# Another written-out step order, with new operation and queue tables, for the opening part of a state-space and gated-MLP kernel

## The chip, the cores and the metric

The kernel runs on one core of one Trainium2 chip. The metric is the device time of one execution in microseconds; the kernel before has a median of 1714.06 us over three executions (1711.05, 1714.14 and 1714.06). The engines are called PE (matrix products), DVE, ACT, POOL and SP in the profile; POOL and SP issue most of the DMAs in the part that changes.

## The reference

A vector `c` makes six rows of modulation. The input `x` (2048 tokens, 576 channels) passes a state-space convolution and then a gated MLP, both with layer norm, modulation and a residual:

```python
mod = (_silu(c) @ w_mod).reshape(c.shape[0], 6, 1, -1)
h = _layernorm(x, axis=-1) * (1 + ca) + sa
P = jnp.exp(logdA[:, :, None] * l[None, None, :])          # 576 x 128 states x 2048 steps
K = jnp.einsum("dn,dnl,dn->dl", Cc, P, dB).real            # one long filter for each channel
x = x + ga * (irfft(rfft(h) * rfft(K)) + h * Dskip)
h = _layernorm(x, axis=-1) * (1 + cb) + sb
z = _gelu(h @ w_in); z1 = z[..., :2304]; z2 = _layernorm(z[..., 2304:])
g = w_sp @ z2 + b_sp
x = x + gb * ((z1 * g) @ w_out)
```

Here `irfft(rfft(...))` stands for the zero-padded Fourier product over 4096 points that the reference spells out.

## The kernel before

The program has three parts: `ssm` makes the filter, convolves, adds the residual and starts the MLP; `phase_a` takes 16 tiles of 128 tokens through the `z2` half of `w_in`; `phase_b` does the gate and the output. The change is in tables that `ssm` reads and in one loop of `phase_a`.

`ssm` consists of small functions, its steps, each issuing a handful of instructions. The list `ORDER` (L186 to L244) names all 1214 of them with their arguments, and the loop at L1003 calls them in that order. A wrapper, `Pin` (L147), keeps every instruction in program order on its engine, so each engine's queue is exactly the list read from left to right; every instruction made that way has line L152 in the profile, and groups are told apart by the names of their tiles. Three more tables belong to it. `GPQ` names the steps whose DMAs are issued by POOL; the others go to SP (`Q`, in `ssm`). `MODE` gives for each of 36 groups of 16 channels the way in which angles are reduced for sine and cosine. `COPY` gives for each group whether DVE ("1") or ACT ("0") copies its filter out of PSUM.

The steps, in the order in which data flows:

- `pole_in`, `pl`, `pload`: the state-space parameters are read, turned into exponents and phases split into bfloat16 parts, stored (`pb_d`, `pa_d`) and read back as `lb`, `lc` and `la`. `m_l`, `m_p`, `m_a`, `m_q`, `m_e`: one row of modulation each, from the load of `w_mod` through 12 products (`ps<-wm,ec`), an ACT copy (`mpart`), two products with `small`, to the result. `st_a`, `st_v`, `ln_r`, `ln_p`, `ln_a`: the layer norm of `x` with a first transform stage, stored to `u1_d`; its output tile is `st1o`.
- For each group: `e_p`, `e_a` (products `sel,lb`, exponential on ACT to `et`); `t_p` (L674, phases by products `sel,lc` and `sel,la`), `t_i`, `t_b` (reduction to a period, tile `ft`), `s_f`, `s_c` (sine and cosine on ACT); `p_a`, `p_b` (two DVE products `pg<-et,ft`) and `p_c` (two more, `et<-ft,et`); `kg_p` (32 matmuls `pk<-pg` and `pk<-et,pg`), `kg_a`, `kg_d`, `k1_p` and `k1_e` (L810, the copy to `k`).
- For each of five blocks of channels `c` and pieces `i`: `u_l`, `u_p`, `u_a` (the transformed input), `z_p` (products of `k` with `cst`), `z_m` (the DVE product `zz<-pk,uu`), `v_p` (products `zz,small`), `v_a` (copy and store to `v_d`). A `z_p` of a block can only come when all groups of that block (eight, in the last block four) have done `k1_e`.
- For each `c` and quarter `q` of the tokens: `y_v` (load of `v_d`; it needs all pieces of that block), `y_x` (load of `x`), `y_p` (L960, eight products with `st`, which are seen as 16 matmuls in the trace), `y_s` (L971, a DVE addition and the store of the new `x`). The data of `y_v.3.0` and `y_v.3.1` lie in `zz` tiles, that of `y_v.4.*` in `uu` tiles, all other in pairs of `u` tiles; block 4 is 64 channels wide, the others are 128 wide.
- `ml.*`, the start of the MLP: `start_load`, `start_sum`, `win_scale`, `start_hi`, `start_lo` for five column blocks of `w_in` (a power-of-two scale from a sum of squares, then a high and a low half-precision part, `wz`, from the tile `wst`); `ln2_stats`, `roots`, `ln2_rows` (second layer norm, tiles `bsx`, `mvx`, `n`), `turn` (transposes `ps<-ident,n` to `nt`), and `z2_mm`, `z2_gelu` of the first token tile (products `pk<-wz,nt`).

How a mode shapes a group's work: in mode 0 PE writes the phases alone, ACT adds a large constant that rounds them, and DVE subtracts (a SCALAR_TENSOR_TENSOR `ft<-ft,ps`) and clears signs. In the other modes PE does the rounding itself by adding and taking off the constant in products with `sel`, so the phases are accumulated twice:

```python
            if MODE[g]:
                magics(2112, True)
                phases((768, 0), False, False)
                magics(2240, False)
                phases((1536, 1792), False, True)
            else:
                phases((768, 0), True, True)
```

After that mode 1 takes a DVE copy and a mask, mode 2 a mask read straight from PSUM, mode 3 an ACT copy and a mask, and mode 4 an absolute value on ACT.

In `phase_a` (L1542) the loop at L1608 takes token tiles 1 to 15. Each has five chunks of products, `z2_mm(b, 0)` to `z2_mm(b, 4)`, each followed by its `z2_gelu`, and between them stand side works from lists (`sides`, called by `do(b, k)`): loads (LD), and the preparation of the other half of `w_in` and of later weights. For tile 1, A0 holds `side_sum(0)`, which squares and sums a block of `w_in` on ACT (`wso<-wst`), and PE holds `win_scale(0)`, which turns that sum into a scale by one small product and DVE work.

Of the kernel before, what the change touches and what calls it, by code (L numbers as in the profile page):

```python
# [170 lines left out]
u_a.1.0 u_a.1.2 u_a.1.4 u_a.2.0 u_a.2.1 u_a.2.3 u_a.2.4 u_a.3.2 u_a.3.4 u_a.3.5 u_a.3.6 u_a.4.0 u_a.4.1 u_a.4.3 u_l.0.0 u_l.0.3 u_l.0.6 u_l.0.7
u_l.1.0 u_l.1.2 u_l.1.3 u_l.1.5 u_l.1.6 u_l.1.7 u_l.2.2 u_l.2.5 u_l.2.6 u_l.2.7 u_l.3.1 u_l.3.2 u_l.3.3 u_l.3.4 u_l.3.6 u_l.4.0 u_l.4.3 v_a.0.2
v_a.0.6 v_a.0.7 v_a.1.1 v_a.1.3 v_a.1.4 v_a.1.5 v_a.1.7 v_a.2.0 v_a.2.1 v_a.2.3 v_a.2.4 v_a.2.5 v_a.3.1 v_a.3.3 v_a.3.4 v_a.3.7 v_a.4.0 v_a.4.1
v_a.4.2 wpre.1 x_l.1 x_l.3 y_s.0.0 y_s.0.1 y_s.1.0 y_s.1.1 y_s.2.1 y_s.2.2 y_s.3.0 y_s.4.0 y_s.4.1 y_s.4.3 y_v.0.0 y_v.0.1 y_v.0.3 y_v.1.0 y_v.1.1
# [4 lines left out]
pole_in.0.5 pole_in.0.4 pole_in.0.2 pole_in.0.1 pole_in.0.0 pl.0.0 pole_in.0.3 pole_in.0.6 pole_in.1.5 pole_in.1.0 pole_in.1.1 pl.0.1 pl.0.2 x_l.0
pl.0.3 pl.0.4 load.msk pl.0.5 pl.0.6 pl.0.11 pl.0.7 pl.0.8 pl.1.0 pl.1.1 pl.0.9 load.c pole_in.1.2 pl.1.2 mod_init st_a.0.0 pl.0.16 pl.0.13 m_l.2  # L180
m_p.2 pl.0.10 pl.0.17 st_a.0.1 st_a.0.2 pl.0.18 pl.0.12 pl.0.14 pl.0.15 m_l.0 m_p.0 st_a.0.3 st_a.0.4 load.small m_a.2 m_q.2 pload.0.0 m_a.0 m_q.0
pl.0.19 pl.0.20 pl.0.21 m_l.1 pl.0.22 pl.0.23 m_e.2 m_e.0 c_l.1 m_p.1 m_a.1 pole_in.1.3 load.sel e_p.1.0 e_p.3.1 pload.0.1 pl.1.11 m_q.1 m_e.1 e_p.4.1
r_l.0 ln_r.0 ln_r.1 e_a.1.0 c_l.0 r_l.1 ln_r.3 e_p.1.1 e_a.1.1 pload.0.2 x_l.1 r_l.2 m_l.3 t_p.1 t_i.1 st_v.1.0 st_v.1.1 t_p.0 load.dsk pole_in.1.4
t_i.0 e_p.2.0 ln_r.2 e_a.2.0 e_p.0.0 e_a.0.0 ln_p.0.0 ln_a.0.0 t_b.0 pole_in.1.6 r_l.3 pl.1.12 ln_p.0.1 t_b.1 s_f.1 ln_a.0.1 pl.1.3 st_v.1.2 pl.1.4
c_l.2 st_v.1.3 st_v.1.4 s_f.0 ln_r.5 ln_p.2.1 ln_a.2.1 ln_r.4 ln_p.2.0 ln_r.6 s_c.0 s_c.1 c_l.3 ln_a.2.0 e_p.0.1 ln_p.4.0 ln_a.4.0 pl.1.5 pl.1.6
e_a.0.1 x_l.2 ln_p.4.1 ln_a.4.1 pl.1.7 m_p.3 pl.1.8 pl.1.9 p_a.0 m_a.3 t_p.2 t_i.2 t_b.2 p_a.1 pl.1.10 p_b.1 p_c.1 ln_r.7 t_p.3 t_i.3 t_b.3 pl.1.16  # L186
s_f.2 p_b.0 p_c.0 kg_p.1 s_c.2 ln_p.6.0 e_a.3.1 ln_a.6.0 kg_a.1 st_v.2.0 st_v.2.1 pl.1.13 st_v.2.2 kg_d.1 e_p.3.0 st_v.2.3 e_a.3.0 m_l.4 e_p.2.1
e_p.5.1 e_a.5.1 ln_p.6.1 e_a.2.1 kg_p.0 ln_a.6.1 t_p.4 pl.1.14 r_l.4 m_q.3 e_a.4.1 t_i.4 kg_a.0 st_v.2.4 m_e.3 c_l.5 r_l.5 ln_r.11 p_a.2 ln_r.8 t_b.4
e_p.7.1 e_p.5.0 kg_d.0 c_l.4 e_a.5.0 e_p.4.0 m_p.4 e_a.4.0 p_b.2 k1_p.0 p_c.2 s_c.4 m_a.4 m_q.4 x_l.3 ln_r.9 s_f.4 k1_e.0 m_l.5 ln_r.10 s_f.3 pl.1.15
m_e.4 kg_p.2 kg_a.2 st_v.3.0 s_c.3 ln_p.8.0 kg_d.2 pl.1.17 st_v.3.1 ln_a.8.0 r_l.7 k1_p.1 e_p.6.1 e_a.6.1 ln_p.8.1 k1_p.2 ln_a.8.1 e_p.7.0 k1_e.2  # L190
e_a.7.0 e_a.7.1 t_p.5 t_i.5 m_p.5 p_a.4 st_v.3.2 k1_e.1 m_a.5 c_l.6 p_a.3 p_b.3 p_c.3 p_b.4 p_c.4 pload.1.0 t_p.7 t_i.7 pload.1.1 kg_p.3 kg_a.3 t_b.5
ln_p.10.0 ln_a.10.0 pl.1.18 t_b.7 s_c.5 ln_p.10.1 r_l.6 ln_a.10.1 pl.1.19 pl.1.20 e_p.6.0 t_p.6 t_i.6 e_a.6.0 s_f.5 st_v.3.3 e_p.9.1 st_v.3.4 e_p.14.1
ln_r.12 t_b.6 s_f.6 m_q.5 m_e.5 s_c.7 ln_r.15 kg_d.3 ln_r.13 s_c.6 p_a.5 kg_p.4 kg_a.4 c_l.7 ln_p.12.0 ln_a.12.0 k1_p.3 k1_e.3 s_f.7 ln_r.14 p_b.5
p_c.5 ln_p.14.1 ln_a.14.1 pl.1.21 pl.1.22 kg_p.5 p_a.6 pl.1.23 ln_p.14.0 ln_a.14.0 kg_a.5 e_a.9.1 ln_p.12.1 ln_a.12.1 e_p.11.1 e_a.11.1 e_p.8.1 turn
e_a.14.1 t_p.8 p_a.7 kg_d.4 pload.2.1 e_p.8.0 e_a.8.0 u_l.0.1 u_l.0.5 e_p.12.1 kg_d.5 u_l.0.4 u_l.0.2 t_i.8 p_b.7 p_c.7 e_a.8.1 e_p.9.0 pload.2.2
e_a.9.0 pload.1.2 p_b.6 p_c.6 t_b.8 s_f.8 k1_p.5 k1_e.5 k1_p.4 k1_e.4 u_l.0.0 s_c.8 t_p.10 t_i.10 t_p.9 t_i.9 cst_l.2 kg_p.6 kg_p.7 t_b.10 t_b.9 p_a.8
s_f.10 cst_l.0 kg_a.6 kg_d.6 s_c.10 kg_a.7 s_f.9 u_p.0.0 u_a.0.0 p_b.8 p_c.8 u_p.0.1 cst_l.1 k1_p.6 k1_e.6 s_c.9 p_a.9 kg_d.7 u_l.1.2 t_p.12 t_i.12
# [12 lines left out]
t_i.18 kg_d.17 t_b.18 s_c.18 s_f.18 u_p.1.4 z_p.1.1 z_m.1.1 kg_p.16 u_a.1.4 kg_p.20 kg_a.20 k1_p.17 s_f.19 k1_e.17 t_p.21 t_i.21 t_p.22 v_p.1.2 s_c.19  # L210
v_a.1.2 p_a.18 p_b.18 p_c.18 t_i.22 z_p.1.0 v_p.1.1 t_b.21 z_m.1.0 s_c.21 u_p.1.3 z_p.1.5 v_a.1.1 kg_a.16 u_l.1.6 s_f.21 u_a.1.3 v_p.1.0 kg_p.18
y_p.0.2 e_p.22.0 t_b.22 s_c.22 s_f.22 v_a.1.0 kg_d.20 e_p.21.0 z_m.1.5 pload.3.0 e_a.21.0 kg_d.16 u_l.1.7 p_a.19 k1_p.16 p_b.19 y_s.0.2 u_l.2.6
kg_a.18 p_c.19 e_a.22.0 k1_p.20 k1_e.20 k1_e.16 kg_d.18 k1_p.18 p_a.21 t_p.23 e_p.24.0 e_a.24.0 k1_e.18 p_b.21 p_c.21 e_p.22.1 e_a.22.1 z_p.1.4
# [2167 lines left out]
```

## Time and profile before

| | |
|---|---|
| median of three executions | 1714.06 us |
| the profiled execution | 1710.31 us |
| its span, first to last instruction | 1708.3 us |
| PE busy | 1644.1 us, 96% |
| DVE, ACT, POOL busy | 1244.0, 834.2, 250.1 us |
| granted PE clock, mean over the span | 0.978 |
| moved by DMA | 376.24 MB, 220 GB/s |

The prediction quotes rows of four kinds. The page's slices cut the span into 40 equal parts of 42.7 us, each a digit for tenths of busy time. A row of windows gives a stretch, its length and the busy time of PE, weight loads, DVE, ACT and POOL with instruction counts, then the granted clock as a share of full speed, the DMA share and GB/s. A row of the timeline gives start, duration (of the whole run of equal instructions), engine, line, operation, output tile, input tiles, shapes and count; the bracket is the engine's idle time before it and what ended that. A row of a group gives a count, then busy time, mean ns of one, and idle time with its releasers. Matmuls in a row overlap in the trace, so the time from one start to the next says more than the sum of durations.

### The profile page before, as it was taken

Reading aid. Unit: us, or ns where it says so; the run is one execution under the profiler, and the core shown is the slowest. Engines: PE = TensorE matmul, PEld = TensorE weight load, DVE = VectorE, ACT = ScalarE, POOL = GpSimd, SP = SyncE. Lnnn points to the kernel's source line nnn. Section 1 sums busy time; section 2 is a strip of 40 time slices with the busy share of each in tenths; the row PEclk is TensorE's granted clock in tenths of the full one; section 3 lists DMA queues with packets and bytes.
Section 4 is the critical chain, followed back from the end, with each engine's and each line's share of the span. In section 5 each row is a group of like instructions: output and inputs, shape, how many; then the busy total and the mean of one; then the engine's idle time right before and its main releaser. Section 6 shows DMA issues by size and latency. Waiting matters only on the chain.

```text
span 1708.3 us, 36473 instructions
## 1 busy us (share of the span) xinstructions
PE 1644.1 (96%) x15254; PEld 1243.3 (73%) x15254; DVE 1244.0 (73%) x2187; ACT 834.2 (49%) x1107; POOL 250.1 (15%) x393
## 2 busy tenths in 40 slices
PE   4778999989999999999999999999999999999999
...
GB/s 227 214 186 236 129 185 228 235 264 269 292 276 253 248 256 285 269 259 265 246 136 263 303 273 257 229 210 174 235 213 229 196 217 110 201 198 215 195 94 43
DMA packets 164645, 376.24 MB, mean 220 GB/s; under 512 B 32961, under 2 KB 80465, under 8 KB 163713
## 3 DMA queue, kind: packets, MB, share of 16 engines
...
HBM read 263.11 MB, written 101.31 MB: 213 GB/s over the span
## 4 chain that ended last, share of the span: by engine, by line
PE 72%; DVE 11%; DMA 3%; issue 3%; ACT 2%; POOL 0%; SPq 0%; ACTq 0%; DVEq 0%; POOLq 0%
PE ps L152 58%; PE pk L152 10%; PE pz L152 5%; DVE gt L152 1%; DVE bsz L152 1%; DVE raw L152 1%; DVE wsp L152 1%; DVE n L152 1%; DVE zset L152 1%; DMA zset<-set_d 1%; DVE wso L152 1%; DVE rq L152 0%; ACT z L152 0%; DMA wst<-in_w_in 0%; DVE ot L152 0%
## 5 line engine op out<-in xcount | busy, mean ns | idle before, releaser
L152 PEld LDWEIGHTS <-zset 128*128 128x128 f16 x7182 | 702.5, 98 | 84.4 <-DMA zset<-set_d 0.9
L152 PE MATMUL ps<-wsp,zset 128*128 128x256 f16 x6048 | 666.5, 273 | 0.6 <-DVE ot L152 0.3
L152 PE MATMUL pz<-wz,nt 128*128 128x512 f16 (+1 forms) x1050 | 207.0, 358 | 0.6 <-ACT nt L152 0.4
L152 ACT ACTIVATE z<-gt 128x1024 f16<-128x1024 f32 x56 | 59.0, 1054 | 282.0 <-DVE gt L152 281.8
L152 PEld LDWEIGHTS <-nt 128*128 128x128 f16 x1120 | 109.0, 98 | 107.5 <-ACT nt L152 1.6
L2086 POOL DMA_DIRECT2D zset<-set_d x96 | 50.8, 530 | 871.8 <-PE ps L152 613.4
L152 DVE SCALAR_TENSOR_TENSOR gt<-ps,sc,bsp 128x512 f32<-128x512 f32 x36 | 27.0, 750 | 201.0 <-PE ps L152 199.3
L152 PE MATMUL ps<-wout,z 128*128 128x288 f16 x1344 | 170.0, 286 | 0.0
L152 PEld LDWEIGHTS <-z 128*128 128x128 f16 x1344 | 131.5, 98 | 33.0
L152 PE MATMUL ps<-n2o,zset 128*128 128x256 f16 x1134 | 128.2, 273 | 0.0
L152 DVE SCALAR_TENSOR_TENSOR gt<-ps,sc,gt 128x512 f32<-128x512 f32 (+1 forms) x180 | 122.2, 696 | 7.9 <-DVE gt L152 0.5
L152 DVE TENSOR_TENSOR raw<-raw 128x256 f32<-128x256 f32 (+2 forms) x226 | 118.0, 528 | 12.1 <-DMA raw<-z_d 7.0
L152 ACT ACTIVATE zset<-raw 128x1792 f16<-128x1792 f32 x47 | 79.6, 1695 | 73.7 <-PE ps L152 46.4
L152 DVE TENSOR_TENSOR zset<-raw,zset 128x1792 f16<-128x1792 f32 x47 | 95.0, 2021 | 21.1 <-ACT zset L152 19.7
L152 DVE TENSOR_TENSOR z<-ps,z 128x512 f32<-128x512 f32 (+1 forms) x126 | 72.0, 599 | 36.8 <-ACT z L152 26.7
L152 DVE TENSOR_TENSOR pg<-et,ft 128x1024 f32<-128x1024 f32 x62 | 74.1, 1216 | 5.8 <-ACT ft L152 3.7
L152 ACT ACTIVATE wsp<-raw,sc 128x1792 f16<-128x1792 f32 x25 | 44.6, 1784 | 52.7 <-DVE raw L152 52.4
L152 PE MATMUL pk<-zz,small 128*128 128x512 f32 x144 | 67.7, 601 | 0.3 <-ACT uu L152 0.3
L152 ACT ACTIVATE z<-z,sc 128x1024 f32<-128x1024 f32 x21 | 24.1, 1148 | 75.6 <-DVE z L152 71.9
L152 ACT ACTIVATE z1b<-gt 128x512 f16<-128x512 f32 (+1 forms) x24 | 17.7, 765 | 87.6 <-DVE gt L152 87.6
L152 ACT ACTIVATE z<-pz,sc 128x512 f32<-128x512 f32 (+1 forms) x90 | 49.2, 578 | 19.6 <-PE pz L152 12.3
L152 PE MATMUL ps<-n2q,wf 128*128 128x512 f16 x252 | 55.9, 379 | 0.0
...
## 6 DMA issues: line engine op xcount, KB each, us to landing
...
```

What stands on the lines that cost most here:

```text
L152: return self.tc.keep_in_program_order(f(*a, **k))
L2086: self.nc.gpsimd.dma_start(o, self.set_d[f, j - 1] if j else self.wa_d[f])
```

## The change

`MODE`, `COPY`, `GPQ` and `ORDER` are replaced. `ORDER` holds the same 1214 names in another sequence. Counts of modes 0 to 4 go from 16, 4, 6, 5, 5 to 18, 3, 5, 4, 6; twelve groups change mode (0: 3 to 0; 9: 2 to 4; 10: 4 to 2; 12: 1 to 2; 15: 4 to 2; 16: 2 to 0; 17: 2 to 1; 18: 4 to 0; 19: 0 to 4; 25: 0 to 4; 26: 1 to 0; 29: 2 to 4). DVE copies 17 filters in place of 14. Nine DMA instructions more are issued by POOL and nine fewer by SP. ACT loads its function tables 36 times in place of 38 in this part. In `phase_a`, for tile 1 alone, `side_sum(0)` moves from ahead of `z2_gelu(1, 0)` to behind `z2_gelu(1, 1)`, and `win_scale(0)` from ahead of `z2_gelu(1, 1)` to behind `z2_mm(1, 2)`.

```diff
-MODE = [int(k) for k in "334133230244121422400000001002000000"]
-COPY = "000011110010001100010000000011011101"
+MODE = [int(k) for k in "034133230424221201040000040004000000"]
+COPY = "100111111001000010000101000110110110"
...
-ml.start_hi.2 y_p.2.2 y_s.2.2 ml.start_lo.2 ml.start_load.4 y_x.1.2 y_v.2.1 y_p.3.0 y_x.3.0 y_s.3.0 y_p.4.0 y_x.3.3 y_s.4.0 ml.ln2_stats.0 ml.roots..0
-y_p.2.1 ml.ld_l y_s.2.1 ml.ln2_rows.0 y_p.1.2 ml.turn.0 y_s.1.2 ml.start_sum.4 ml.two y_x.4.2 ml.turn_hi.0 ml.z2_mm.0.0.0 y_v.3.2 ml.turn_lo.0 y_v.3.1
...
+ml.ap ml.start_lo.1 ml.start_hi.2 y_x.4.2 ml.start_lo.2 y_p.1.2 y_v.2.1 y_v.4.3 y_p.2.2 y_p.3.0 y_v.3.2 y_s.2.2 y_p.4.0 ml.start_load.4 y_x.2.1
+y_p.4.3 y_x.4.0 y_s.3.0 y_s.4.0 y_s.1.2 ml.ln2_stats.0 ml.roots..0 y_x.3.2 y_x.3.1 ml.ln2_rows.0 y_s.4.3 y_p.2.1 y_p.3.2 ml.two y_v.4.1 ml.az y_v.3.1
...
             self.z2_mm(b, 0)
-            do(b, A0)
+            if b > 1:
+                do(b, A0)
             self.z2_gelu(b, 0)
...
-            do(b, PE)
+            if b > 1:
+                do(b, PE)
             self.z2_gelu(b, 1)
+            if b == 1:
+                do(b, A0)
             self.z2_store(b - 1)
...
             self.z2_mm(b, 2)
+            if b == 1:
+                do(b, PE)
             self.z2_gelu(b, 2)
```

Three places show what the new list does to the queues. The first is PE's queue from the last `v_p` (`zz,small`) to the first product of the first token tile (`wz,nt`). `acc,ones` are the sums of `win_scale`; `u,st`, `zz,st` and `uu,st` are `y_p`; where rows are left out, the pair of `u` rows alternates, eight rows to one `y_p`. Before:

```order
1602 L152 MATMUL pk<-zz,small 128x512 x4
1603 L152 MATMUL pk<-acc,ones 128x1 x2
1604 L152 MATMUL pk<-u_4327,st_2315 64x128
1605 L152 MATMUL pk<-u_4328,st_2315 64x128
...
1612 L152 MATMUL pk<-zz,st_2315 64x128 x8
1613 L152 MATMUL pk<-uu,st_2315 64x64 x8
1614 L152 MATMUL pk<-u_4826,st_2315 64x128
...
1622 L152 MATMUL pk<-u_4716,st_2315 64x128
...
1630 L152 MATMUL ps<-ident,n_4883 128x128 x5
1631 L152 LDWEIGHTS nt
1632 L152 MATMUL pk<-wz,nt 128x512
```

And now:

```order
1577 L152 MATMUL pk<-acc,ones 128x1
1578 L152 MATMUL pk<-zz,small 128x512 x2
1579 L152 MATMUL pk<-u_4769,st_2009 64x128
...
1587 L152 MATMUL pk<-u_4334,st_2009 64x128
...
1595 L152 MATMUL pk<-zz,st_2009 64x128 x8
1596 L152 MATMUL pk<-uu,st_2009 64x64 x16
1597 L152 MATMUL pk<-u_4801,st_2009 64x128
...
1605 L152 MATMUL pk<-u_4825,st_2009 64x128
...
1613 L152 MATMUL ps<-ident,n_4882 128x128 x5
1614 L152 LDWEIGHTS nt
1615 L152 MATMUL pk<-wz,nt 128x512
```

Before, y_p.2.2, 3.0, 4.0, 2.1 and 1.2 stand there, one of them ahead of the `zz` rows; now 1.2, 2.2, 3.0, 4.0, 4.3, 2.1 and 3.2, two of them ahead.

The second place is DVE's queue to the same transposes, whose input is `n`. `wz<-wst` are `start_lo`, `xb`, `xz` and `x1l` the additions of `y_s`, `bsx` and `mvx` the statistics, `rq` and `rx` the inverse root. Before:

```order
505 L152 TENSOR_TENSOR xb<-pk,xb 128x512
506 L152 SCALAR_TENSOR_TENSOR wz<-wst,sc,wz 128x4x512
507 L152 TENSOR_SCALAR wz<-wst,sc 128x512
508 L152 SCALAR_TENSOR_TENSOR wz<-wst,sc,wz 64x512
509 L152 TENSOR_TENSOR xz<-pk,xz 128x4x128
510 L152 TENSOR_TENSOR xz<-pk,xz 128x4x64
511 L152 BN_STATS bsx<-xz 128x6 x2
...
522 L152 SCALAR_TENSOR_TENSOR rx<-rq_4860,rx 128x1
523 L152 TENSOR_TENSOR xb<-pk,xb 128x512
524 L152 SCALAR_TENSOR_TENSOR n_4883<-xz,mvx,mrow 128x576
525 L152 SCALAR_TENSOR_TENSOR n_4883<-n_4883,rx,mrow 128x576
```

And now:

```order
510 L152 SCALAR_TENSOR_TENSOR wz<-wst,sc,wz 128x4x512
511 L152 TENSOR_SCALAR wz<-wst,sc 128x512
512 L152 SCALAR_TENSOR_TENSOR wz<-wst,sc,wz 64x512
513 L152 SCALAR_TENSOR_TENSOR wz<-wst,sc,wz 128x4x512
...
516 L152 TENSOR_TENSOR xb<-pk,xb 128x512
517 L152 TENSOR_TENSOR xz<-pk,xz 128x4x128
518 L152 TENSOR_TENSOR xz<-pk,xz 128x4x64
519 L152 TENSOR_TENSOR xb<-pk,xb 128x512
520 L152 BN_STATS bsx<-xz 128x6 x2
...
531 L152 SCALAR_TENSOR_TENSOR rx<-rq_4868,rx 128x1
532 L152 SCALAR_TENSOR_TENSOR n_4882<-xz,mvx,mrow 128x576
```

The second `xb` addition has moved from behind the inverse root to ahead of the statistics (and is now that of y_s.1.2, y_s.2.1 having gone behind `n`), and two `start_lo` stand together.

The third place is DVE's queue at the 17th and 18th product `zz` of the convolution; `pg` and `et<-ft,et` are `p_a`, `p_b` and `p_c` of one group. Before, 44 `pg` products precede the 18th `zz`, counted from the start of the queue:

```order
378 L152 TENSOR_TENSOR zz<-pk,uu 128x1024
379 L152 TENSOR_TENSOR xb<-pk,xb 128x512
380 L152 SCALAR_TENSOR_TENSOR et<-ft,et 128x16x32
381 L152 TENSOR_TENSOR et<-ft,et 128x16x32
382 L152 TENSOR_TENSOR zz<-pk,uu 128x1024 x2
383 L152 TENSOR_TENSOR pg<-et,ft 128x1024 x2
```

And now 48 do:

```order
386 L152 TENSOR_TENSOR zz<-pk,uu 128x1024
387 L152 TENSOR_TENSOR pg<-et,ft 128x1024 x2
388 L152 SCALAR_TENSOR_TENSOR et<-ft,et 128x16x32
389 L152 TENSOR_TENSOR et<-ft,et 128x16x32
390 L152 SCALAR_TENSOR_TENSOR ft<-ft,ps 128x1024
391 L152 TENSOR_SCALAR ft<-ft 128x1024
392 L152 TENSOR_TENSOR kab<-kab,dsk 128x4
393 L152 TENSOR_TENSOR pg<-et,ft 128x1024 x2
394 L152 SCALAR_TENSOR_TENSOR et<-ft,et 128x16x32
395 L152 TENSOR_TENSOR et<-ft,et 128x16x32
396 L152 TENSOR_TENSOR zz<-pk,uu 128x1024
```

Between the two products there now stand the DVE works of two groups. Ahead of the first `zz` 20 `pg` products stand in both; ahead of the 24th 55 before and 54 now.

More of the change, by code (lines that the diff above doesn't have):

```diff
@@ L171 @@
[L171 to L174, printed above, removed]
@@ L177 @@
+y_x.1.3 y_x.2.0 y_x.2.2 y_x.2.3 y_x.3.0 y_x.3.1 y_x.3.2 y_x.3.3 y_x.4.1 y_x.4.2
 """.split()
 ORDER = """
[L179 to L181 removed]
@@ L182 @@
[L182 to L197, printed above, removed]
@@ L210 @@
[L210 to L213, printed above, removed]
@@ new lines @@
+pl.0.11 pole_in.1.0 pl.0.5 x_l.0 st_a.0.0 pl.0.6 pl.0.7 st_a.0.1 pl.0.12 load.small st_a.0.2 st_a.0.3 pl.0.8 st_a.0.4 pl.0.9 pl.0.10 pl.0.13
+pole_in.1.1 pl.0.16 pl.0.17 m_l.2 pl.0.18 pl.1.0 m_p.2 m_a.2 m_q.2 pl.0.19 pl.0.20 pl.0.14 m_l.0 m_p.0 m_a.0 pl.0.15 m_l.1 pl.1.1 m_e.2 pole_in.1.2
+pl.0.21 pl.0.22 m_q.0 pl.0.23 r_l.1 m_e.0 c_l.0 m_p.1 load.sel m_a.1 m_q.1 pload.0.0 pl.1.2 pl.1.11 e_p.0.0 e_a.0.0 m_e.1 ln_r.0 ln_r.1 pole_in.1.4
+pload.0.1 ln_r.2 pload.0.2 x_l.1 ln_r.3 pole_in.1.3 e_p.1.0 e_a.1.0 e_p.2.0 e_a.2.0 c_l.1 pole_in.1.5 r_l.2 pole_in.1.6 t_p.0 t_i.0 r_l.5 t_p.1 t_b.0
```

113 lines of the change are left out of this document (68 added, 45 removed).

## The prediction

> **What bounds the kernel now.** I read the busy shares and slices first, then busy time by stage up to 440 us, then the waits, the timeline of the one long hole, and the groups of instructions. From the page, engine totals and slices of 43 us each:
>
> ```profile
> span 1708.3 us, 36473 instructions
> PE 1644.1 (96%) x15254; PEld 1243.3 (73%) x15254; DVE 1244.0 (73%) x2187; ACT 834.2 (49%) x1107; POOL 250.1 (15%) x393
> PE   4778999989999999999999999999999999999999
> ```
>
> TensorE (PE) is idle for 1708.3 − 1644.1 = 64.2 us, and its low digits are the first slices and the ninth, which is the hand-over to the MLP. Busy time by stage (columns: window, length, PE, weight loads, DVE, ACT, POOL, granted clock, DMA share, GB/s):
>
> ```profile
> 0.00:60.00 60.00, 32.45 (x214) 12.94 (x215) 37.32 (x122) 36.91 (x66) 24.28 (x43) 0.84 0.88 237
> 60.00:150.00 90.00, 71.75 (x1136) 39.60 (x1137) 82.14 (x158) 80.78 (x111) 25.64 (x40) 0.75 0.66 204
> 150.00:370.00 220.00, 215.85 (x3142) 142.49 (x3139) 197.75 (x264) 196.99 (x264) 69.62 (x103) 1.00 0.73 206
> 370.00:394.00 24.00, 16.06 (x117) 11.91 (x116) 19.94 (x50) 9.40 (x13) 11.33 (x16) 0.79 0.77 234
> 394.00:440.00 46.00, 44.96 (x318) 25.07 (x317) 43.02 (x119) 24.76 (x38) 16.59 (x22) 1.00 0.93 287
> ```
>
> Length less PE gives idle times of 27.55, 18.25, 4.15, 7.94 and 1.04 us: 58.9 of the 64.2 us lie before 440 us, where nearly all of the change is. From 0 to 60 the kernel waits for loads and short chains; from 60 to 150 DVE and ACT are both about 90% busy and PE is not the bound; from 150 to 370 PE is the bound (98%), with DVE and ACT close behind (90%); from 370 to 394 one chain of latencies leads to the first token tile. So PE work taken out of 150 to 370 counts in full, and the other gain is in filling or shortening the 7.94 us. The hand-over, from PE's waits and the timeline (start, duration, engine; in brackets the idle time before and what ended it):
>
> ```profile
> PE pk L152 <- DMA zz<-v_d: 5.3, 2, 4.5
> 376.14 1.09 PE L152 MATMUL pk<-u,st 128*64 128x128 f32 x16
> 381.71 0.59 PE L152 MATMUL pk<-zz,st 128*64 128x128 f32 x2 [4.48 <-DMA zz<-v_d]
> 384.65 1.27 PE L152 MATMUL pk<-uu,st 128*64 128x64 f32 x14
> 387.89 3.68 PE L152 MATMUL pk<-u,st 128*64 128x128 f32 x30 [1.31 <-DMA u<-v_d]
> 389.90 0.69 DVE L152 TENSOR_TENSOR xb<-pk,xb 128x512 f32<-128x512 f32 x1 [0.63 <-PE pk L152]
> 390.51 0.81 DVE L152 SCALAR_TENSOR_TENSOR n<-xz,mvx,mrow 128x576 f32<-128x576 f32 x1
> 392.23 0.77 PE L152 MATMUL ps<-ident,n 128*128 128x128 f32 x5 [0.66 <-DVE n L152]
> 412.17 0.63 PE L152 MATMUL pk<-uu,st 128*64 128x64 f32 x16
> ```
>
> The last v leaves, is stored and read back; PE has one `u,st` block (1.09 us) to do meanwhile and then waits 4.48 us. The result goes through `xz`, statistics and `n` on DVE to the transposes. The sum is made against the profiled execution: span 1708.3 us, 1710.31 us in all, so 2.0 us lie outside. It is 3.75 us below the median shown (1714.06); I take a difference of spans as the same difference of medians.
>
> **The change part by part.** *A: fewer phase matmuls.* A group in mode 0 needs neither the two `sel` passes nor a second pass of `lc` and `la`. Groups 0, 16, 18 and 26 go to mode 0 and 19 and 25 leave it: net two fewer. One whole group with them, at full clock:
>
> ```profile
> 109.37 0.39 PE L152 MATMUL ps<-sel 48*128 48x512 bf16 x2
> 109.59 0.27 PE L152 MATMUL ps<-sel,lc 48*128 48x256 bf16 x2
> 109.70 0.27 PE L152 MATMUL ps<-sel,la 48*128 48x256 bf16 x2
> 109.81 0.38 PE L152 MATMUL ps<-sel 48*128 48x512 bf16 x2
> 110.03 0.27 PE L152 MATMUL ps<-sel,lc 48*128 48x256 bf16 x2
> 110.14 0.27 PE L152 MATMUL ps<-sel,la 48*128 48x256 bf16 x2
> 110.34 0.32 PE L152 MATMUL pk<-pg 128*32 128x64 f32 x8
> ```
>
> These overlap, so starts count: 110.34 − 109.37 = 0.97 us for six pairs, of which the two `sel` pairs take 0.22 each and an `lc`+`la` pass 0.21, together 0.65. Of the net two, group 0 falls in the first 150 us, where PE waits anyway. A is −0.65 us; bounds −1.3 (both count) and 0.
>
> *B: work of DVE and ACT.* From the groups up to 440 us (count, then busy us and mean ns):
>
> ```profile
> L152 DVE COPY k<-pk 128x512 f32<-128x512 f32 x14 | 9.5, 685 | 1.6 <-PE pk L152 1.6
> L152 ACT ACTIVATE k<-pk 128x512 f32<-128x512 f32 x22 | 13.2, 615 | 1.8 <-PE pk L152 1.8
> L152 ACT ACT_TABLE_LOAD x38 | 48.8, 1283 | 3.4 <-DVE ft L152 2.1 <-PEq L2370 0.7
> L152 ACT ACTIVATE ft<-ps,consts_s 128x1024 f32<-128x1024 f32 x16 | 17.9, 1127 | 2.5 <-PE ps L152 2.5
> L152 DVE SCALAR_TENSOR_TENSOR ft<-ft,ps 128x1024 f32<-128x1024 f32 x16 | 19.4, 1214 | 1.0 <-PE pk L152 1.0
> L152 DVE TENSOR_SCALAR ft<-ps 128x1024 int32<-128x1024 int32 x6 | 7.3, 1219 | 2.2 <-PE ps L152 2.1
> L152 DVE COPY ft<-ps 128x1024 f32<-128x1024 f32 x4 | 4.9, 1218 | 0.0
> ```
>
> DVE takes 3 more k copies, 3 × 0.685 = +2.06; the modes cancel on it (2 × 1.214 more, 1.218 and 1.219 less). ACT gives up 3 × 0.615 and two table loads of 1.283 and takes 2 × 1.127: −2.16. Both engines are hidden by PE from 150 to 370, so B is 0, with those two as bounds (−2.16, +2.06).
>
> *C: the hand-over.* Between the last `zz,small` and the transposes PE now has seven y_p blocks, before five. The two new ones are y_p.3.2, a `u,st` block of 1.09 us, and y_p.4.3, a `uu,st` block of 0.63 us. Before, both stood behind 394 us, where PE is 98% busy, so moved into the hole they save 1.72 us. None lengthens the chain: y_p.1.2 now stands ahead of the `zz,st` block and fits into the 4.48 us; y_p.4.3, y_p.2.1 and y_p.3.2 stand behind the block whose result is awaited, while DVE needs from about 385.1 to 392.2 for it. On DVE, the addition of y_s.2.1 (wait 0.63, work 0.69) leaves its place ahead of `n`, and y_s.1.2 (0.69, nothing to wait for, its block being done long before) comes in ahead of the statistics: −1.32 + 0.69 = −0.63. The two low parts of `wz`, before apart, now stand together ahead of the first of these additions; DVE has the time in which PE waits for the transfer. C is −1.72 − 0.63 = −2.35 us. Its lower bound is the whole hole, −7.94. Its upper: both new blocks held on the chain at the low clock, at 3.68 / 2 = 1.84 and 1.27 × 16/14 = 1.45: +3.3.
>
> *D: the front.* The steps up to the first token are all reordered and nine more DMAs issue from POOL, nine fewer from SP (POOL is 40% busy to 60 us and 28% to 150 us). What bounds this part, 60 to 150 us, is DVE and ACT, and their queue to the first `zz` product is of one length: it is preceded by the same 20 `pg` products before and now. One wait there, and one kind of block:
>
> ```profile
> PE ps L152 <- ACT st1o L152: 3.9, 3, 2.3
> 37.95 2.12 PE L152 MATMUL ps<-mpart,small 128*128 128x288 f32 x4
> ```
>
> I take 0. Bounds: −3.9 if the three waits for `st1o` before 60 us go, +2.12 if the second step of one modulation row, four matmuls like these, comes to stand on the way to the first `e_p`: m_q.1 is now ahead of it, as m_p.1 was already.
>
> *E: side sums.* In the second tile, side_sum 0 moves behind gelu 1 and win_scale 0 behind the third chunk of matmuls:
>
> ```profile
> 418.40 2.34 ACT L152 ACTIVATE wso<-wst 128x2560 f16<-128x2560 f32 x1 [6.58 <-DVE mvx L152]
> 410.00:420.00 10.00, 10.00 (x116) 6.81 (x114) 9.34 (x27) 2.58 (x3) 1.51 (x2) 1.00 0.95 295
> ```
>
> Behind the 2.34 us on ACT queue the evictions of that tile's first chunk. PE is busy for all of the 10 us around it, so an earlier eviction wins nothing: 0. If PE's cover were gone, the eviction ahead of it would be up to 2.34 earlier.
>
> Sum: −0.65 + 0 − 2.35 + 0 + 0 = −3.0 us, 1705.3 for the span and 1714.06 − 3.0 = **1711.1 us** for the time.
>
> **The rivals.** *Clock.* After the 4.48 us wait the granted clock is low until the transposes:
>
> ```profile
> 381.80:392.00 10.20, 7.65 (x64) 6.30 (x64) 8.18 (x21) 1.22 (x2) 5.85 (x9) 0.50 0.88 258
> ```
>
> With y_p.1.2 ahead of it the wait is 4.48 − 1.09 = 3.39 us. If the clock then stays up, the two blocks on the chain take 1.09 + 0.63 and not 1.84 + 1.45: −1.6 more, 1709.5. No row has a wait between this and 4.48 us in a busy stretch, so the trace cannot say. [...] From the one wait that the trace has, I give it 0.13.
>
> *A shorter front.* The `st1o` waits go: −3.9 more, 1707.2. For it speaks that PE, at 54% before 60 us, has room; against, that the 82.14 us of DVE work behind it stays. Chance 0.14.
>
> *No change.* The new blocks' loads come too late for the hole, or the saving on DVE is eaten by the two low parts of `wz` (some 3.5 us each: 2.34, 0.48, 0.75). Only A is left: 1713.4. Chance 0.16.
>
> *Slower: DVE becomes the bound from 150 to 370.* Ahead of the 18th `zz` product now stand 48 `pg` products, before 44, two whole groups more. A group on DVE is at least:
>
> ```profile
> L152 DVE TENSOR_TENSOR pg<-et,ft 128x1024 f32<-128x1024 f32 x62 | 74.1, 1216 | 5.8 <-ACT ft L152 3.7 <-ACT et L152 1.5 <-PE pk L152 0.5
> L152 DVE SCALAR_TENSOR_TENSOR et<-ft,et 128x512 f32<-128x512 f32 x31 | 21.4, 690 | 0.9
> L152 DVE TENSOR_TENSOR et<-ft,et 128x512 f32<-128x512 f32 x31 | 21.2, 684 | 0.0
> ```
>
> 2 × 1.216 + 0.690 + 0.684 = 3.8 us, so 7.6 us for two. DVE's idle time in the stage is 220 − 197.75 = 22.25 us, but part of it is waiting for ACT's `ft` and `et`, which no order fills. If none of the 7.6 is absorbed, PE runs out of products: +7.6 − 3.0, 1718.7. It decides once more than 3.0 of the 7.6 us fall on PE. Against it: later on, before the 24th product, the count is 54 against 55, so the lead is made good. Chance 0.24.
>
> **How the numbers follow.** Two measurements of this kernel can be told apart from about 0.2%, 3.4 us; my sum of −3.0 lies just inside. The forecast has 0.33, and by the bounds of A and C 0.15 of that is faster and 0.18 the same. Faster: 0.15 + 0.13 + 0.14 = 0.42. Same: 0.18 + 0.16 = 0.34. Slower: 0.24. The range runs from 1704.0, where front and clock gain together leave 0.08 below, to 1720.0, which is the slower case and a little; some 0.12 of it, B's and D's upper bounds with it, lies beyond.
>
> **What would show it.** Right: PE idle of about 5.6 us in the hand-over, seven y_p blocks ahead of the transposes, the wait for `zz<-v_d` near 3.4 us, the `xb` wait of 0.63 gone; the first `wz,nt` at about the same place in PE's work. Clock case: granted clock 1.00 through the hand-over. Front case: idle PE before 60 us under 24 us. Slower case: PE idle from 150 to 370 above 8 us, with `DVE zz` as what ended it. Wrong altogether, if the time goes anywhere behind 440 us.

## The result, and the profile after

The changed kernel is slower: 1728.46 us (median of six executions, 1723.86 to 1732.28) against 1713.11 us for the kernel before (six, 1707.79 to 1714.99). The ratio is 1.0093, with a 95% interval of 1.007 to 1.0115: 15.4 us, where 3 us less had been forecast, and outside the range. Its profiled execution took 1729.27 us.

The page of the changed kernel, engine totals:

```profile
span 1727.5 us, 36453 instructions
PE 1648.8 (95%) x15238; PEld 1239.5 (72%) x15238; DVE 1244.3 (72%) x2190; ACT 832.1 (48%) x1104; POOL 255.8 (15%) x402
```

DVE and ACT are about as busy as they were (1244.0 and 834.2 us before). PE is idle for 78.7 us, 14.5 more, and busy for 4.7 us more, with 16 matmuls fewer (15238 against 15254) and a mean granted clock of 0.973 against 0.978. To see where, both executions are cut at the same points of the work: the first `u,small`, the end of the last `zz,small`, the first transposes of the first token tile, the first `pz` product of tile 1, and 25 to 30 us on. Stages of the kernel before (columns as in the prediction):

```profile
130.00:146.20 16.20, 12.93 (x227) 7.85 (x218) 13.23 (x18) 15.18 (x21) 6.36 (x10) 0.68 0.85 253
146.20:375.87 229.67, 225.52 (x3206) 148.24 (x3198) 206.03 (x273) 205.25 (x274) 71.51 (x106) 1.00 0.73 209
375.87:392.23 16.36, 9.11 (x85) 7.53 (x84) 13.71 (x44) 3.96 (x4) 8.76 (x13) 0.69 0.76 229
392.23:415.04 22.81, 21.08 (x194) 13.05 (x194) 21.48 (x55) 7.83 (x12) 11.63 (x16) 1.00 0.98 291
415.04:440.00 24.96, 24.96 (x131) 12.75 (x130) 23.24 (x70) 17.90 (x28) 6.41 (x8) 1.00 0.89 277
```

And of the changed kernel, with its first 60 us:

```profile
0.00:60.00 60.00, 29.08 (x206) 11.15 (x207) 38.86 (x125) 37.83 (x67) 15.81 (x29) 0.80 0.85 234
130.00:149.50 19.50, 13.20 (x281) 8.48 (x280) 14.40 (x21) 12.83 (x18) 5.28 (x8) 0.63 0.71 216
149.50:385.27 235.77, 230.09 (x3190) 146.77 (x3190) 205.36 (x287) 206.42 (x275) 75.36 (x114) 0.99 0.71 202
385.27:403.71 18.44, 9.82 (x113) 8.20 (x112) 13.57 (x29) 2.49 (x2) 13.80 (x19) 0.81 0.93 276
403.71:425.23 21.52, 20.01 (x163) 11.68 (x163) 20.48 (x52) 8.86 (x14) 9.93 (x15) 1.00 0.79 242
425.23:455.00 29.77, 26.48 (x124) 12.85 (x122) 24.70 (x74) 17.75 (x26) 7.33 (x10) 0.89 0.80 241
```

Idle time (length less PE) rises from 27.6 to 30.9 us before 60 us, from 3.3 to 6.3 around 130 to 150, from 4.2 to 5.7 from there to the last `zz,small`, from 7.3 to 8.6 in the hand-over, and from 0 to 3.3 in tile 1. Three of these have a few rows each behind them.

**A hole at 133 to 140 us.** From the timeline of the changed kernel, ACT, PE and POOL:

```profile
139.80 0.60 ACT L152 ACTIVATE wst<-pk 128x512 f32<-128x512 f32 x1 [6.20 <-DMA pa_d<-pt]
140.45 0.59 PE L152 MATMUL pk<-sel,lb 112*128 112x512 bf16 x1 [5.04 <-ACT wst L152]
130.92 3.73 POOL L152 DMA_DIRECT2D pa_d<-pt  x6 [5.25 <-DVE pt L152]
```

ACT stands for 6.2 us ahead of one exponential, since its output tile `wst` must wait until the last terms of the poles, issued from 130.9 to 134.7, have been stored. (The step `turn` closes the pool that holds their tile `pt` and opens the one that `wst` is taken from.) PE runs out of work behind it, and both lose the time in the stage that they bound.

**The hand-over.** First the chain before, then the chain now:

```profile
375.90 0.60 ACT L152 ACTIVATE uu<-pk 128x512 f32<-128x512 f32 x1 [1.07 <-PE pk L152]
376.80 0.54 POOL L152 DMA_DIRECT2D v_d<-uu  x1 [1.11 <-ACT uu L152]
379.44 1.15 SPq L152 DMA_DIRECT2D uu<-v_d  x2
385.95 0.42 DVE L152 TENSOR_TENSOR xz<-pk,xz 128x256 f32<-128x256 f32 x1 [0.16 <-PE pk L152]
```

```profile
385.36 0.60 ACT L152 ACTIVATE v<-pk 128x512 f32<-128x512 f32 x1 [1.34 <-PE pk L152]
386.25 0.56 POOL L152 DMA_DIRECT2D v_d<-v  x1 [3.32 <-ACT v L152]
388.21 0.40 PE L152 MATMUL pk<-u,st 128*64 128x128 f32 x2 [2.93 <-DMA u<-v_d]
390.32 0.92 SPq L152 DMA_DIRECT2D uu<-v_d  x2
394.86 0.30 PE L152 MATMUL pk<-uu,st 128*64 128x64 f32 x2 [2.09 <-DMA uu<-v_d]
397.00 1.12 PE L152 MATMUL pk<-uu,st 128*64 128x64 f32 x16 [1.84 <-DMA uu<-v_d]
398.15 0.42 DVE L152 TENSOR_TENSOR xz<-pk,xz 128x256 f32<-128x256 f32 x1 [4.27 <-PE pk L152]
403.71 0.77 PE L152 MATMUL ps<-ident,n 128*128 128x128 f32 x5 [0.34 <-DVE n L152]
```

From the copy of the last v to the second `xz` addition it takes 398.15 − 385.36 = 12.8 us, before 385.95 − 375.90 = 10.05. From there to the transposes it takes 403.71 − 398.15 = 5.56, before 392.23 − 385.95 = 6.28. The store and the load in the middle are slower (issues by median time to landing; the first two rows are of the kernel before, the next two of the changed one):

```profile
v_d<-uu POOLq DMA_DIRECT2D x1, 256.0 KB, 2.5
uu<-v_d SPq DMA_DIRECT2D x2, 128.0 KB, 4.1
```

```profile
v_d<-v POOLq DMA_DIRECT2D x1, 256.0 KB, 3.8
uu<-v_d SPq DMA_DIRECT2D x2, 128.0 KB, 5.3
```

**The side sums of tile 1.** In the changed kernel:

```profile
435.83 2.32 ACT L152 ACTIVATE wso<-wst 128x2560 f16<-128x2560 f32 x1
438.30 0.59 PE L152 MATMUL pz<-acc,ones 128*128 128x1 f32 x2 [3.29 <-ACT wso L152]
435.00:440.00 5.00, 1.72 (x7) 0.88 (x7) 1.61 (x5) 4.62 (x8) 1.54 (x2) 0.78 1.04 381
440.00:445.00 5.00, 5.00 (x16) 1.94 (x15) 4.56 (x18) 2.69 (x5) 0.57 (x1) 0.54 0.95 252
```

PE has done the third chunk at 435.0, but the small product of `win_scale` that now follows it needs the sum, which ACT has only begun. PE stands for 3.29 us, and behind that its clock is 0.54 from 440 to 445 us.

### The profile page after: what moved, and what is told of

The parts are those of the page before. It is cut to its first block, busy times and chain, and to the rows that moved or that the text cites. A ratio compares the mean times of both kernels' runs of the same rounds, so it can differ in the third digit from the quotient of the medians.

```text
span 1727.5 us, 36453 instructions
## 1 busy us (share of the span) xinstructions
PE 1648.8 (95%) x15238; PEld 1239.5 (72%) x15238; DVE 1244.3 (72%) x2190; ACT 832.1 (48%) x1104; POOL 255.8 (15%) x402
## 4 chain that ended last, share of the span: by engine, by line
PE 65%; DVE 8%; DMA 5%; issue 2%; ACT 1%; POOL 0%; SPq 0%; DVEq 0%; POOLq 0%; ACTq 0%
PE ps L152 55%; PE pz L152 8%; PE pk L152 2%; DMA zset<-set_d 1%; DVE gt L152 1%; DVE raw L152 1%; DVE wsp L152 1%; DMA u<-v_d 1%; DVE zset L152 1%; DVE bsz L152 1%; DVE n L152 1%; DMA n_d<-nt 0%; DMA gbs<-in_w_out 0%; DVE rq L152 0%; DMA uu<-v_d 0%
## 5 line engine op out<-in xcount | busy, mean ns | idle before, releaser
L152 DVE BATCH_NORM_STATS2 bsz<-z 128x6 f32<-128x384 f32 x96 | 49.3, 549 | 9.2 <-ACT z L152 8.6
```

Of the source, the lines that this page charges most:

```text
L152: return self.tc.keep_in_program_order(f(*a, **k))
```

## The experiments

The expectations speak of the "base" and of ratios; every ratio below is against the kernel before on the same chip, with its 95% interval, from five rounds.

**The side sums alone**: the kernel before with the five changed lines of `phase_a`; and the changed kernel without them.

> The kernel before, with only the move of the second tile's side sums. Theory (read from the two traces): the sum on ACT ends after PE has done the third chunk, and the sum's small product, now behind that chunk, stops PE for about 3.3 us, after which it runs some 5 us at half clock; so about 6 us slower than before, near 1719 us, with an idle stretch of about 3 us ended by ACT wso. Rival (the prediction's term E): the move costs nothing, 1713 us, no such wait.

> The changed kernel with that move undone. Theory: 6 us faster than the changed kernel, near 1722 us, and still some 9 us slower than before. Rival: all of the loss is in the step order and the time stays at 1728 us.

Measured: 1.0025 (1.0013 to 1.0036), 1716.69 us; and 1.0048 (1.0028 to 1.0069), 1720.03 us, against 1.0093 with the move. The wait stands in the first kernel too:

```profile
PE pz L152 <- ACT wso L152: 2.7, 1, 2.7
425.00:430.00 5.00, 2.34 (x12) 0.97 (x11) 1.70 (x4) 4.50 (x8) 1.71 (x2) 0.95 0.98 349
430.00:435.00 5.00, 5.00 (x25) 2.65 (x24) 4.55 (x19) 3.28 (x6) 0.56 (x1) 0.71 1.04 340
```

The theory holds in both directions, and its 6 us came out as 0.25% or 4.3 us when added, 0.45% or 7.7 us when taken away, 0.2% or 3.4 us in a third pair below. From the first `pz` to the last transposes of tile 15 the profiles have 191.6 to 192.7 us without the move and 195.2, 196.2 and 198.3 us with it. In the shortest of these three, the run with the move and a later exponential below, PE waits as long but its clock stays up:

```profile
431.34 0.38 PE L152 MATMUL pz<-acc,ones 128*128 128x1 f32 x2 [3.27 <-ACT wso L152]
431.34:436.34 5.00, 5.00 (x31) 3.08 (x32) 4.03 (x16) 3.46 (x8) 0.56 (x1) 1.00 1.05 304
```

So part of the price, the low clock behind the wait, differs from one profile to the next: 0.54, 0.71 and 1.00.

**The hole**: one exponential of the changed kernel later.

```diff
-... e_p.14.1 pl.1.22 ... turn u_l.0.1 p_c.5 e_a.14.1 kg_p.5 ... k1_p.4 e_a.10.1
+... pl.1.22 ... turn u_l.0.1 p_c.5 kg_p.5 ... k1_p.4 e_p.14.1 e_a.14.1 e_a.10.1
```

> The changed kernel with one exponential moved: the steps e_p.14.1 and e_a.14.1, which write a tile (wst) that lies in memory from which the last pole terms are still being stored, come six ACT instructions later, just ahead of e_a.10.1. Theory: the hole at 133 to 140 us, in which ACT waits 6.2 us for the store pa_d<-pt and PE 5.0 us for ACT, shrinks to 2 us or so and the time falls by 3 to 5 us, to about 1724 us. Rival: what bounds the front is the sum of DVE and ACT work, the same wait comes back at the next such tile, and the time stays within 1.5 us of the changed kernel.

> The changed kernel with two edits: no move of the side sums, and the exponential of the group 14 six ACT instructions later, as in the third experiment. Theory: the two losses are separate and add up, 7 and 6 to 8 us off 1728: a ratio of 1.000 to 1.002 to before, 1711 to 1715 us. Rival: they overlap (PE waits later for something else), and it stays at 1.004 or above.

Measured: 1.0054 (1.0036 to 1.0073) with the side sums moved, 0.39% below the changed kernel; and 1.0034 (1.0019 to 1.0049) without, 0.14% below the run without the move (these two intervals overlap). On average some 4.5 us. In the second profile the stage reads

```profile
130.00:143.00 13.00, 12.28 (x228) 7.61 (x219) 10.82 (x15) 9.93 (x12) 2.22 (x4) 0.61 0.86 255
143.00:380.40 237.40, 231.17 (x3190) 147.14 (x3190) 205.65 (x287) 205.84 (x275) 75.12 (x114) 0.99 0.70 201
```

with 0.7 us idle in the first row, and the last `zz,small` ends at 380.4 us, and not at 382.7 to 387.0 as where the exponential is not moved. Undoing both takes off 0.59%, undoing one of them 0.39% or 0.45%, so the losses add up only roughly, and the second kernel, called the kernel of 1.0034 below, is still 0.34% slower than before.

Is it the store? The last pole steps earlier, everything else in place:

```diff
-... t_b.6 s_f.6 m_e.5 pl.1.16 pl.1.17 pl.1.18 s_c.6 ... pl.1.19 pl.1.20 ... pl.1.21 ... pl.1.22 ... pl.1.23 p_b.5 turn
+... t_b.3 pl.1.16 ... kg_d.2 pl.1.17 ... ln_a.10.0 pl.1.18 ... ln_a.10.1 pl.1.19 pl.1.20 ... s_c.6 pl.1.21 pl.1.22 pl.1.23 ... turn
```

> The changed kernel without the side sums' move (1.0048 of before), the exponentials all in their place, but with the last pole steps (pl.1.16 to pl.1.23) earlier, so that their terms are stored well ahead of the step turn. Theory: the wait of ACT at 133 to 140 us is for that store, so it is gone here too and the ratio falls to 1.002 to 1.0035, as with the later exponential. Rival: it is the memory of other early tiles, the wait stays within 1 us of 5 on PE and the ratio at 1.005.

Measured: 1.0072 (1.006 to 1.0084), no faster than its base (1.0028 to 1.0069) and probably slower. The wait is gone, from ACT's timeline:

```profile
123.86 1.02 ACT L152 ACTIVATE ft<-ps 128x1024 f32<-128x1024 f32 x1 [3.88 <-DVE ft L152]
136.52 1.19 ACT L152 ACTIVATE st1o<-ps 128x576 f32<-128x576 f32 x2 [3.00 <-DMA u_d<-st1o]
140.58 0.62 ACT L152 ACTIVATE wst<-pk 128x512 f32<-128x512 f32 x1
```

So the releaser was read rightly: with the store done, nothing is waited for at `wst`. But now ACT waits 3.88 us for `ft` from DVE, in whose queue the pole work stands earlier, and 3.00 us for another store; the base has neither wait. The wait was right, the gain was not. Moving the exponential later paid here; moving the store earlier did not.

**Order and tables crossed.** The order of before up to `turn` with the rest of the new one and the new tables; the new order, modes and copies with the old queue table; and the kernel before with the new queue table.

> The order of before up to the step turn (about 145 us), then what is left in the order of the changed kernel, with the changed tables of modes, copies and queues and without the move of the side sums. Theory: the loss before the first token tile arises ahead of about 180 us, so this comes to 1713 to 1716 us, 7 to 9 us under the changed kernel without the side sums' move. Rival (the prediction's slower case): the order of DVE's work from 150 to 370 us loses the time, and this stays near 1722 us.

> The changed kernel without the side sums' move, and with the queue table of before (which steps' DMAs POOL issues, which SP); order, modes and copies stay the new ones. It stands against the same kernel with the new queue table, 1.0048 of before. Theory: the 3.4 us more of PE idle in the first 60 us come with the queue table, since the first hybrid had them too with the order of before; so 3 to 4 us less, a ratio near 1.0025, and idle time of about 28 us before 60 us. Rival: they come with the order (one row of modulation finished ahead of the first exponential); idle time stays near 31 us and the ratio at 1.005.

> The kernel before with the new queue table alone. Theory: the queue table is fitted to its order, and in the front it costs 4 us by itself and up to 9 more from 60 to 130 us, as in the first hybrid: 1716 to 1724 us, idle PE of 31 us to 60 us. Rival: the queues are not at fault, the hybrid lost by the modes or at its joint; this then stays within 2 us of before, with 27 to 28 us of idle PE to 60 us.

Measured: 1.0089 (1.0073 to 1.0105), 1.0263 (1.0238 to 1.0287) and 1.0283 (1.0258 to 1.0307). Neither of the theories had any of the three within its numbers. A queue table and an order that were not made for each other cost 37 us in the second (against its own base, 1.0048) and 48 us in the third. Waits of PE for loads of the convolution and of v in the second and third:

```profile
PE pk L152 <- DMA u<-u_d: 16.4, 3, 9.6
```

```profile
PE pk L152 <- DMA u<-v_d: 7.5, 2, 6.4
PE pk L152 <- DMA zz<-v_d: 7.0, 1, 7.0
```

The rows show which loads PE waited for, not what made them late; that they stood behind others' waits in their queues was the author's guess. Since a crossing costs this much by itself, the first of the three says nothing of the front of the new order, and the difference between the kernels cannot be split between order and queues.

**The front.** Edits on the kernel of 1.0034: three loads later on SP, the layer-norm sums behind the poles, and both; then the modulation products as before, on the kernel with the later loads; and the reverse on the kernel before.

```diff
-... m_e.1 ln_r.0 ln_r.1 pole_in.1.4 pload.0.1 ln_r.2 pload.0.2 x_l.1 ln_r.3 pole_in.1.3 ... pole_in.1.5 r_l.2
+... m_e.1 ln_r.0 ln_r.1 pload.0.1 ln_r.2 pload.0.2 ln_r.3 ... pole_in.1.5 r_l.2 x_l.1 pole_in.1.4 pole_in.1.3
...
-... x_l.0 st_a.0.0 pl.0.6 pl.0.7 st_a.0.1 pl.0.12 load.small st_a.0.2 st_a.0.3 pl.0.8 st_a.0.4 pl.0.9
+... x_l.0 pl.0.6 pl.0.7 pl.0.12 load.small pl.0.8 pl.0.9 st_a.0.0 ... pl.0.17 st_a.0.1 st_a.0.2 ... pl.0.15 st_a.0.3 st_a.0.4
```

> The changed kernel without the side sums' move and with the later exponential of group 14 (1.0034 of before), and with three loads on SP (x_l.1, pole_in.1.4 and pole_in.1.3) put behind r_l.2. In the changed kernel they issue at 35 to 36.5 us, together with the load of lb that the first exponential waits for, which then takes about 6 us where it took 2.7. Theory: lb lands 3 us earlier, the first e_p starts near 38 us and not 41, idle PE to 60 us falls from 32 to 29, and the time by 2 to 3 us, a ratio near 1.002. Rival: the front is bound by work of DVE and ACT, and the same time is lost by 130 us; ratio 1.0034.

> The same base, with the four layer-norm sums st_a.0.0 to st_a.0.3 put behind the pole steps, much as before; in the changed kernel they stand ahead of the exponentials of the poles on ACT, which start at 18.5 us and not at 11.3. Theory: the chain of the poles is the way to the first e_p; it comes 3 to 5 us earlier, idle to 60 us falls to about 28, the time by 3 us, a ratio of 1.001 to 1.002. Rival: the first e_p is late only by the loads beside lb, and this stays at 1.0034 with e_p near 41 us.

> Both front edits, of the loads and of the pole steps, on the same base. Theory: if each removes a part of the same lateness of the first e_p, both give not more than the better one and 1 us, idle PE to 60 us is 27 to 28 as before and the ratio 1.000 to 1.001. Rival: the front was not the cause, and the ratio is 1.003 or more.

> The base of the run with later loads (1.0024 of before), with the modulation products on PE in the order of before: m_q.2 behind m_p.0, m_q.1 behind the first exponential's products. Theory: the PE waits for mpart, 8.5 us in the changed order and 0.8 before, are the lateness of the front; they fall to some 2 us, idle PE to 60 us to 27 to 28, the ratio to 1.000 to 1.001. Rival: DVE gets the rows of modulation no later in the changed kernel than before (31.6 and 39.4 us against 31.4 and 40.1), so these waits cost nothing and the ratio stays at 1.0024.

> The kernel before, with the modulation products in the changed order: m_a.2 and m_q.2 ahead of m_p.0, and m_q.1 ahead of the first exponential's products. Theory: 3 to 4 us slower, a ratio of 1.002, idle PE to 60 us of 30 to 31. Rival: as for the run above, nothing, 1.000 and 25 to 28 us.

Measured, in this order: 1.0024 (1.0011 to 1.0037), 1.0045 (1.0033 to 1.0057), 1.0056 (1.0039 to 1.0072), 1.0039 (1.0024 to 1.0054) and 0.9997 (0.9988 to 1.0007). The later loads bring the first exponential's products from 41.1 to 39.2 us, and 0.1% of time, which the intervals don't tell from nothing. The poles first make it worse: the modulation's copies then come later on ACT, and those products start at 45.8 us. The last run decides. From its profile:

```profile
0.00:60.00 60.00, 26.83 (x205) 11.41 (x213) 36.07 (x117) 35.20 (x64) 23.79 (x42) 0.83 0.85 232
149.30:376.20 226.90, 224.96 (x3202) 148.16 (x3198) 204.72 (x271) 204.76 (x273) 72.03 (x106) 1.00 0.73 209
```

PE is idle for 33.2 us in the first 60, more than in the changed kernel, and yet this kernel takes the time of before and ends its last `zz,small` at 376.2 us: the idle time comes back later. PE's idle time before 60 us is slack there, and the 3.4 us more of it in the changed kernel need not cost anything.

**The hand-over.** The changed kernel without the side sums' move and without the two new blocks there; and the kernel before with what the prediction valued.

```diff
-... y_v.2.1 y_v.4.3 ... y_p.3.0 y_v.3.2 ... y_p.4.3 ... y_s.4.3 y_p.2.1 y_p.3.2 ... ml.z2_mm.0.0.0 ... ml.z2_mm.0.1
+... y_v.2.1 ... y_p.3.0 ... y_p.2.1 ... ml.z2_mm.0.0.0 y_v.3.2 y_v.4.3 ... ml.z2_mm.0.1 y_p.3.2 y_p.4.3 y_s.4.3
...
-... y_p.2.2 ... y_p.3.0 ... y_s.4.0 ml.ln2_stats.0 ml.roots..0 y_p.2.1 ml.ld_l y_s.2.1 ml.ln2_rows.0 y_p.1.2 ml.turn.0 y_s.1.2
+... y_p.1.2 y_p.2.2 ... y_p.3.0 y_v.3.2 ... y_s.4.0 y_s.1.2 ml.ln2_stats.0 ml.roots..0 y_p.2.1 y_p.3.2 ml.ld_l ml.ln2_rows.0 y_s.2.1 ml.turn.0
```

> The changed kernel without the side sums' move, and with the two new blocks of the hand-over (loads y_v.3.2 and y_v.4.3, products y_p.3.2 and y_p.4.3, and the addition y_s.4.3) put back behind the first products of the first token tile. Theory: their loads share the DMA engines with the store and the load that the chain waits for, which took 1.3 and about 1.5 us longer; from the last v to the transposes it takes 16 to 17 us in place of 19, 1.7 us of PE work come back later, and the time falls by 0.5 to 1.5 us, hardly to be told from none. Rival: the chain is late by its own place in its queue; the stretch stays at 19 us, and the time is 1.7 us longer.

> The kernel before, with only the hand-over as the prediction valued it: the addition y_s.2.1 behind the rows of the layer norm, y_s.1.2 ahead of its statistics, the block y_p.1.2 ahead of the awaited one, and the block y_p.3.2 with its load in the hole. Prediction's term: 1.1 + 0.6 = 1.7 us faster, 1710 us, a ratio of 0.999. Rival: the load of the new block beside those that the chain waits for takes it back, and the ratio is 1.000 or above.

Measured: 1.0062 (1.0045 to 1.0078) and 1.0036 (1.0024 to 1.0048), the second clearly slower than the kernel that it came from, the first (from 1.0048) within the noise. From the first profile:

```profile
382.70:398.80 16.10, 6.80 (x82) 5.97 (x81) 13.59 (x29) 2.48 (x2) 10.64 (x15) 0.82 0.91 273
398.80:423.70 24.90, 24.21 (x194) 14.19 (x195) 21.56 (x54) 8.96 (x14) 12.86 (x19) 0.84 0.84 256
```

Without the new blocks the hand-over takes 16.1 us against 19.1, as the theory expected; but the next stage takes 24.9 against 21.2, part of it at a low clock, and the time is not shorter, as the theory had it, but 2.4 us longer, if the difference of the ratios is taken (the intervals overlap). From the second, whose stretch is 20.6 us long and not 16:

```profile
385.24 1.53 POOL L152 DMA_DIRECT2D u<-v_d  x2
389.08 0.69 DVE L152 TENSOR_TENSOR xb<-pk,xb 128x512 f32<-128x512 f32 x1 [5.43 <-DMA xb<-in_x]
389.98 2.61 PE L152 MATMUL pk<-u,st 128*64 128x128 f32 x16 [3.98 <-DMA u<-v_d]
394.29 1.33 PE L152 MATMUL ps<-ident,n 128*128 128x128 f32 x5 [1.71 <-DVE n L152]
```

The moved addition waits 5.4 us for its `x`, the new block 4.0 us for its v, whose load is issued at 385.2. Each stands ahead of the chain in its queue and so becomes part of it. No version tried beats the kernel before.

## Why the prediction was wrong

Stage lengths over the profiles give the account. Runs with the order of before are the kernel before, the one with the side sums, the one with the modulation reversed and, in the first and last row, the one with the new hand-over. Runs with the new order and tables are the changed kernel, the one without the side sums' move, in the first row also the one without the new blocks, and from the second row on the two with the later exponential.

| stage | order of before | new order | difference |
|---|---|---|---|
| to the end of the last `zz,small` | 375.9, 377.5, 376.2, 373.7 | 385.3, 387.0, 382.7 | +9.2 |
| the same, with the later exponential | as above | 380.0, 380.4 | +4.4 |
| from there to the first transposes | 16.4, 15.4, 15.6 | 18.4, 19.1, 16.8, 18.1 | +2.3 |
| to the first `pz` | 22.8, 22.8, 24.3 | 21.5, 21.2, 21.5, 21.2 | −2.0 |
| to the last transposes of tile 15, side sums as before, or moved | as before: 192.1, 192.7 | moved: 198.3, 195.2; 196.2 in the kernel before with the move | +4.2 |
| to the end | 1101.2, 1102.4, 1102.4, 1104.6 | 1103.9, 1103.7, 1104.2, 1104.6 | +1.5 |

Differences are between means. All but the second row, which is a part of the first, sum to 15.2 us against 15.4 measured, which is closer than single profiles let one expect: the same order varies by 4 us in the first row from one profile to the next, so its difference, and all the smaller ones, are rough.

- **E, the side sums, at 0, failed** by 3.4 to 7.7 us in three pairs of runs, the clearest step. It read that PE was busy around `wso` and that an earlier eviction wins nothing, and stopped there. It costed one of the two moved steps, the sum on ACT, and not the other, `win_scale`, which issues a product on PE. That product waits for the sum (3.29 us), and the rest of the tile's products stand behind it.
- **D, the front, at 0**, was right on what it named: the modulation's order, priced at up to 2.12 us, costs nothing (0.9997). But "a queue of one length" is not a queue without holes. One exponential writes memory that a store is still reading, so that ACT waits 6.20 us, and that costs about 4.5 us. Its upper bound had no such wait in it. Some 4.4 us more in that row have no cause that a run shows; the crossings could not isolate it, since order and queues cannot be parted. The traces give a lead. From the first `u,small` to the last `zz,small` it takes 226.8 to 230.5 us in the four profiles with the order of before, and 233.2 to 238.2 us in the five of the new order in the first two rows, the exponential later or not. In four of these five PE waits 2.2 to 4.5 us for a load of `u`, in none of the first four. In the changed kernel the clock behind that wait is 0.50 from 168.5 to 171 us (0.83 over 165 to 175 us, before 1.00):

```profile
168.51 2.05 PE L152 MATMUL pk<-u,small 128*128 128x512 f32 x2 [2.79 <-DMA u<-u_d]
```

  The fifth waits 0.5 us for that load, keeps a clock of 1.00 and still takes 233.2 us, and no run removes the wait alone, so this stays open.
- **C, the hand-over, at −2.35**, had its two gains about right: the chain on DVE became 0.72 us shorter (0.63 forecast) and the next stage 1.3 us in these two profiles, 2.0 between the means (1.72 forecast). It left out that the store and the load of the chain itself might become slower, as they did (3.8 and 5.3 us, before 2.5 and 4.1): +2.7 us from the copy of v to the second `xz`. Of its signs the seven blocks came and the wait at `xb` went, but PE is idle for 8.6 us and not 5.6: the block put ahead waits 2.93 us for its own load and the awaited one 2.09 and 1.84 us. In the table the two stages come to +0.3 together. It had called the new blocks free since "none lengthens the chain" by its place on PE. In the run without them the load takes 4.4 us and the way from the copy to the second `xz` 10.4, against 5.9 and 13.2 us in the run that it came from; but the two runs with the later exponential need only 11.1 and 10.7 us with the blocks in place, so how much the blocks' loads take isn't settled.
- **B** was right on the time: ACT's busy time fell by 2.1 us (2.16 forecast) and no time follows from it; only DVE's total rose by 0.3 and not by 2.06. **A** was not tested alone; the 16 matmuls fewer are its two groups of eight, but PE's busy time rose all the same.
- **The slower rival**, DVE behind from 150 to 370 us at +7.6, is not what happened. Idle time from the first `u,small` to the last `zz,small` rose from 4.2 to 5.7 us, of which `DVE zz` ended 1.0 and the load of `u` above 2.8. Its sign was right for another reason.
- **The clock rival** did not come: after waits of 2.93, 2.09 and 1.84 us PE's clock was low in the hand-over again, only later (0.53 from 399 to 404 us). No run shows a length of wait below which the clock stays up. Nor did the shorter front: PE is idle for 30.9 us before 60 us, where it asked for under 24.

```profile
395.00:399.00 4.00, 1.44 (x20) 1.11 (x21) 0.85 (x2) 0.00 (x0) 1.57 (x4) 0.73 1.03 297
399.00:404.00 5.00, 4.66 (x49) 4.26 (x50) 4.55 (x18) 0.00 (x0) 4.43 (x6) 0.53 0.93 285
```

- **"Wrong altogether, if the time goes anywhere behind 440 us"**: hardly. The queues there are unchanged word for word, and the +1.5 us in the last row is no more than the runs with the order of before vary (1101.2 to 1104.6).
